# Convolution stem with group norm, forward and gradients: the operand tiles of the input gradient turned by DMA for the weight gradient

## The chip, the cores and the metric

One core of a Trainium2 chip runs the whole program. The metric is the device time of one launch in microseconds (us), for which several runs give a median. A profile shows one execution in detail: TensorE (PE) does the matmuls, with weight loads (PEld) beside them; VectorE (DVE), ScalarE (ACT) and GpSimd (POOL) do the rest; SyncE (SP) does nothing but issue DMA transfers, one after another, and the waits ahead of each. SPq in a profile row is SP's instruction queue; the length of such a row is the time that SP needs to issue the transfer, not the transfer.

## The reference

A strided convolution (31 taps, stride 2, 256 to 256 channels, 2 x 16000 positions), a normalisation over the positions of each channel, GELU, and the gradients of all four inputs:

```python
B, T, D, K = 2, 16000, 256, 31
def _fwd_reference(x, w, gn_gamma, gn_beta):
    s = 2
    L = (T - K) // s + 1
    h = jnp.einsum('blc,cd->bld', x[:, 0:s * L:s, :], w[0])
    for i in range(1, K):
        h = h + jnp.einsum('blc,cd->bld', x[:, i:i + s * L:s, :], w[i])
    mu = jnp.einsum('bld->bd', h)[:, None, :] / L
    var = jnp.einsum('bld->bd', (h - mu) ** 2)[:, None, :] / L
    h = (h - mu) / jnp.sqrt(var + 1e-5)
    h = h * gn_gamma[None, None, :] + gn_beta[None, None, :]
    return _gelu(h)
def reference(x, w, gn_gamma, gn_beta, grad_out):
    _out, _vjp = jax.vjp(_fwd_reference, x, w, gn_gamma, gn_beta)
    return (_out, *_vjp(grad_out))
```

The outputs are out_0 (the activations), out_1 (gradient of x), out_2 (gradient of w), out_3 and out_4 (of gamma and beta).

## The kernel before

All three convolutions (forward, input gradient, weight gradient) are done by a fast algorithm that splits a product of two pairs into three products, A, B_ and C_, of sums or differences of operands, three levels deep. A first-level choice is called a branch (`br`), the second a leaf (`lf`); the third lies inside the matmul groups.

The stages follow one another on TensorE: the forward (L815), the input gradient (L1363), the weight gradient (L1653). GELU and its derivative (`gelu_batch`) of one batch run beside the convolutions of the other.

The input gradient (`input_grad`, L1423) runs over 2 batches, 4 chunks of 512 positions of the folded gradient, 3 branches and 2 halves (`pr`) of a chunk. For a chunk, `e_load` fetches dy and h, `e_comp` makes the gradient rows `EG` out of them, and `e_spread` copies them into `ET` with the margins. `g_sums` builds the operands of a branch on DVE: `first` makes the branch's two rows in `GS`, `second` the leaves A and C_ in `GL` (two buffers, used by turns), `third` and `outer` the third level. Chunks from (0, 3) on take `split` (36 matmuls of 512 columns for each branch and half), the earlier ones `plain` (44).

The weight gradient (`weight_grad`, L1738) goes through nine combinations of branch and leaf (`COMBOS`). Each takes four tiles of x (`x_tile`, 1 MB) and one tile of gradient rows for each batch (`d_tile`, `D2`, with rows as partitions and channels as columns, so the transposed form of what the input gradient uses). These rows are prepared during the input gradient: `dn_turn` (L1311) turns `EG` by two DMA transposes of 512 KB for each chunk and stores the result to `dn_d`; `d2_piece` (L1533) loads pieces of `dn_d` back, forms the first- and second-level differences on DVE (`sub`, L1549) and stores them to `d2_d`, from which `d_tile` loads.

The order of all work is worked out before the launch by `Plan`: every operation is recorded with an engine, an estimated length and what it depends on; two passes give it a due time, to which `self.lead` adds a number for each kind of operation, and a list schedule gives every engine's program order. Each engine, SP too, then executes its list strictly in that order. The estimate for a DMA transpose on SP is in `turn` (L612):

```python
np_ = nbytes / 256
add("SP", 0.15 + 0.00105 * np_, [out], [in_],
    lambda: nc.sync.dma_start_transpose(out=out, in_=in_), dma=np_ * PK[256] / 16e3 * 1.03, ns=PK[256], tp=SH[256], slack=slack)
```

A transpose of 256 KB is issued by `gelu_unit` (two for each unit of batch 0), and one of 32 KB by `dgb_store` for the gradients of gamma and beta. Nearly all DMA transfers go through SP, whether the code says SP or POOL (`load`, L602, sends everything over 4 KB there).

Of the kernel before, what the change touches and what calls it, by code (L numbers as in the profile page):

```python
# [21 lines left out]
ORDER = (B_, A, C_)  # L22
COMBOS = ((A, A), (A, C_), (A, B_), (C_, B_), (B_, B_), (B_, A), (B_, C_), (C_, A), (C_, C_))
# [15 lines left out]
class Plan:  # L39
# [3 lines left out]
    def __init__(self, tc):  # L43
# [11 lines left out]
            "F0 conv_stem_kernel wrapper": 5.6,  # L55
            "F0 f_evac last": -3.2,
            "F0 f_join f_evac": -10.3,
            "F0 f_join split": 14.0,
            "F0 f_mm f_three_ac": -0.4,
            "F0 f_mm f_three_b": 1.0,  # L60
            "F0 f_three_b split": -3.7,
            "F0 keep f_evac": -3.1,
            "F0 keep split": -17.8,
            "F0 load conv_stem_kernel": 58.4,
            "F0 load f_evac": -14.0,
            "F0 load put": 0.6,
            "F0 load x_pre": 3.5,
            "F0 load_gb conv_stem_kernel": -25.1,
            "F0 tt f_sums": -15.0,
            "F0 tt second": 4.0,  # L70
            "F0 tt third": -5.9,
            "F0 turn w2_part": -0.5,
            "F0 turn x_load": -4.6,
            "F0 w_sub w2_part": -5.7,
            "F0 x_pre conv_stem_kernel": 1.3,
            "F0 zero conv_stem_kernel": 0.9,
            "F0 zero f_evac": -7.8,
            "F0 zero w2_part": -33.8,
            "F0 zero x_load": -111.5,
            "F0a f_evac last": -19.8,  # L80
            "F0a f_join f_evac": 0.7,
            "F0a f_join f_first": -11.0,
            "F0a f_join split": 28.3,
            "F0a f_mm f_leaf": -8.4,
            "F0a f_mm f_three_ac": 0.2,
            "F0a f_mm f_three_b": -5.0,
            "F0a f_mm pe_turn": -48.4,
            "F0a f_three_b f_first": -12.7,
            "F0a f_three_b split": -30.8,
            "F0a keep f_first": -31.2,  # L90
            "F0a keep split": -10.0,
            "F0a load load_w": 58.4,
            "F0a load x_load": 82.3,
            "F0a load x_pre": 55.5,
            "F0a put x_first": -19.2,
            "F0a tt f_sums": -12.3,
            "F0a tt second": -19.7,
            "F0a tt third": -13.9,
            "F0a turn x_load": -48.2,
            "F0a w_sub f_first": -12.5,  # L100
            "F0a x_pre conv_stem_kernel": 13.3,
            "F0a zero load_w": 14.3,
            "F1 f_evac last": 4.0,
            "F1 f_join f_evac": 11.4,
            "F1 f_mm f_leaf": 0.7,
            "F1 f_mm f_three_b": 1.8,
            "F1 f_three_b plain": -0.7,
            "F1 f_three_b split": -2.0,
            "F1 gelu_batch conv_stem_kernel": -6.7,
            "F1 gelu_unit gelu_batch": 0.7,  # L110
            "F1 keep f_evac": -0.4,
            "F1 keep plain": -0.3,
            "F1 keep split": -34.2,
            "F1 load f_evac": 0.5,
            "F1 load gelu_unit": 3.0,
            "F1 load out0_store": -3.7,
            "F1 tiny elem_finalize": -260.7,
            "F1 tiny fwd_stats": 2.5,
            "F1 tt f_sums": -15.6,
            "F1 tt second": -1.3,  # L120
            "F1 tt third": 0.6,
            "F1 turn gelu_batch": 0.5,
            "F1 turn gelu_unit": 3.7,
            "F1 turn x_load": 1.8,
            "F1 zero gelu_batch": -52.4,
            "F1z f_evac last": -7.1,
            "F1z f_join f_evac": -5.3,
            "F1z f_join split": -17.5,
            "F1z f_mm f_leaf": -2.5,
            "F1z f_mm f_three_ac": 0.6,  # L130
            "F1z f_mm f_three_b": -0.3,
            "F1z f_three_b split": 2.4,
            "F1z keep f_evac": 7.0,
            "F1z keep split": -160.7,
            "F1z load f_evac": 7.0,
            "F1z tt f_sums": -20.3,
            "F1z tt second": -3.1,
            "F1z tt third": -0.7,
            "F1z turn x_load": 8.8,
            "F1z w_sub f_again": -0.3,  # L140
            "F1z zero f_evac": -10.2,
            "F1z zero x_load": -6.0,
            "G0 e_add e_comp": 3.6,
            "G0 e_comp conv_stem_kernel": -3.2,
# [6 lines left out]
            "G0 g_three_b split": 5.1,  # L151
# [4 lines left out]
            "G0 load e_load": -6.2,  # L156
            "G0 spread e_spread": -288.3,
            "G0 tt first": -2.4,
            "G0 tt outer": 17.1,
            "G0 tt second": -7.8,  # L160
            "G0 tt third": 14.0,
            "G0 turn dn_turn": -10.7,
            "G0 zero e_comp": -37.5,
            "G0 zero e_spread": 69.3,
            "G0a e_add e_comp": -0.5,
            "G0a e_comp conv_stem_kernel": -5.0,
            "G0a e_spread conv_stem_kernel": -1.4,
            "G0a g_join last": -0.9,
            "G0a g_mm g_leaf": 1.6,
            "G0a g_mm g_three_ac": 2.7,  # L170
            "G0a g_mm g_three_b": 2.3,
            "G0a g_three_b plain": 0.6,
            "G0a gelu_batch conv_stem_kernel": -22.1,
            "G0a gelu_unit gelu_batch": 0.3,
            "G0a keep last": 3.8,
            "G0a keep plain": -2.4,
            "G0a load dgb_store": 91.4,
            "G0a load dn_turn": -2.4,
            "G0a load e_load": 11.2,
            "G0a load g_store": 9.1,  # L180
            "G0a load gelu_unit": 4.5,
            "G0a load load_w2": -6.9,
            "G0a spread e_spread": -45.7,
            "G0a tiny elem_finalize": -2.2,
            "G0a tiny fwd_stats": -186.8,
            "G0a tt first": 20.5,
            "G0a tt gelu_unit": -0.6,
            "G0a tt second": -4.2,
            "G0a tt third": 1.7,
            "G0a turn dgb_store": -3.7,  # L190
            "G0a turn gelu_batch": -1.8,
            "G0a w_sub w2_sub": 2.0,
            "G0a zero conv_stem_kernel": -104.8,
            "G0a zero e_spread": -148.7,
            "G0a zero gelu_batch": -5.4,
            "G1 e_add e_comp": -0.5,
            "G1 e_comp conv_stem_kernel": 1.5,
            "G1 e_spread conv_stem_kernel": 0.2,
            "G1 g_join last": 1.0,
            "G1 g_join split": 4.3,  # L200
            "G1 g_mm g_three_ac": -2.1,
            "G1 g_mm g_three_b": -0.3,
            "G1 g_three_b split": -150.3,
            "G1 keep last": -1.0,
            "G1 keep split": 1.0,
            "G1 load d2_piece": 0.8,
            "G1 load dn_turn": -4.2,
            "G1 load e_load": -1.5,
            "G1 spread e_spread": 0.2,
            "G1 sub d2_piece": 0.3,  # L210
            "G1 tt first": 2.1,
            "G1 tt outer": 6.2,
            "G1 tt second": 7.7,
            "G1 tt third": 8.8,
            "G1 turn dn_turn": 0.4,
            "G1 zero e_comp": -0.2,
            "G1 zero e_spread": -0.6,
            "G1z g_join last": -4.0,
            "G1z g_join split": -7.1,
            "G1z g_mm g_three_b": 4.9,  # L220
            "G1z g_three_b split": 5.3,
            "G1z keep split": 7.7,
            "G1z load g_store": 15.8,
            "G1z tt first": -1.8,
            "G1z tt outer": 23.1,
            "G1z tt second": -0.8,
            "G1z tt third": -0.3,
            "W keep w_done": -6.2,
            "W keep weight_grad": -417.1,
            "W leaf_d weight_grad": -3.3,  # L230
            "W load d_tile": 1.3,
            "W load w_done": -3.6,
            "W load w_out": 16.2,
            "W load weight_grad": -11.1,
            "W load x_raw": 16.8,
            "W load x_tile": 6.5,
            "W pair_d weight_grad": 1.6,
            "W pair_x weight_grad": 0.5,
            "W w_add weight_grad": 1.8,
            "W w_add x_tile": -5.4,  # L240
            "W w_mm w_pairs": -3.1,
            "W w_mm w_single": -13.7,
            "W w_pairs weight_grad": -117.4,
            "W w_sum w_done": 3.8,
            "Wa keep w_done": 24.4,
            "Wa keep weight_grad": -116.9,
            "Wa leaf_d weight_grad": -12.3,
            "Wa load d_tile": 22.3,
            "Wa load out0_late": 20.9,
            "Wa load x_raw": 2.8,  # L250
            "Wa pair_d weight_grad": -4.4,
            "Wa pair_x weight_grad": -7.3,
            "Wa turn out0_late": -45.0,
            "Wa w_add weight_grad": 19.2,
            "Wa w_mm w_pairs": -39.5,
            "Wa w_mm w_single": -2.9,
            "Wa w_pairs weight_grad": 10.2,
            "Wa w_sum w_done": 24.8,
# [269 lines left out]
def conv_stem_kernel(  # L528
# [13 lines left out]
    nc = tc.nc  # L542
# [875 lines left out]
    def w2_outer():  # L1418
        for lf in (A, C_):
            for br in ORDER:  # L1420
                w2_sub(MIR[br], MIR[lf])
# [507 lines left out]
```

## Time and profile before

| what | us |
|---|---|
| median of the runs | 1114.31 (1112.18 to 1119.1) |
| profiled execution | 1114.1 |
| its span | 1112.1 |
| PE / DVE / ACT busy | 1082.7 / 993.1 / 609.6 |
| input gradient, first to last matmul begins | 412.2 to 819.1 |
| weight gradient | 819.8 to 1107.7 |

The page's slices of the span (40 of 27.8 us each; a digit is the busy share in tenths):

```profile
PE   5999999999999999999999998999999999999998
...
DVE  6995958789998997999999979979689989999996
...
DMA  9589999976969799889775999999789555796883
```

TensorE is busy nearly everywhere but in the first slice. The chain that ended last is short, since PE rarely waited for anything: its pieces are the last matmuls and the eviction after them.

### The profile page before, as it was taken

The page shows a single profiled execution, that of the slowest core. Times are in us where ns is not written, and L with a number is a line of the kernel's source. Part 1 is how long each engine was busy: PE and PEld are TensorE (multiplying, and loading weights), DVE is VectorE, ACT ScalarE, POOL GpSimd, SP SyncE. Part 2 cuts the span into 40 slices and gives each one's busy share as a digit, 9 for nine tenths or more (in the row PEclk, how much of TensorE's full clock was granted, in tenths as well). Part 3 has the DMA queues.
Part 4 walks back from the last instruction along what each step waited for, and adds up shares of the span by engine and source line. Part 5 has one row for each costly group of instructions (what it writes and reads, how often), then busy time and mean ns, then how long its engine had stood idle before and what let it go on. Part 6 is the DMA issues. An engine that isn't in the chain of part 4 may idle for free. (4 is left out here: it accounts for less than half of the span.)

```text
span 1112.1 us, 19739 instructions
## 1 busy us (share of the span) xinstructions
PE 1082.7 (97%) x8132; PEld 796.3 (72%) x8132; DVE 993.1 (89%) x1026; ACT 609.6 (55%) x854; POOL 11.0 (1%) x27
## 2 busy tenths in 40 slices
PE   5999999999999999999999998999999999999998
PEld 4888889988888984444444443444468888888887
DVE  6995958789998997999999979979689989999996
ACT  2253434588887659797866766665642323322332
POOL 0000000000000000000000000000000000000000
PEclk9999999999999999999999999999999999999999
DMA  9589999976969799889775999999789555796883
GB/s 227 66 220 225 242 272 272 253 151 167 190 202 186 204 334 313 203 254 276 191 245 159 280 330 295 289 301 311 247 277 270 181 194 146 262 333 205 277 255 101
DMA packets 346893, 261.47 MB, mean 235 GB/s; under 512 B 187702, under 2 KB 315572, under 8 KB 340916
## 3 DMA queue, kind: packets, MB, share of 16 engines
q1 hardware_dynamic: 346612, 260.22, 83.8%
q8 instruction: 63, 1.03, 0.4%
q14 instruction: 26, 0.21, 0.1%
q0 software_dynamic: 192, 0.00, 0.0%
HBM read 120.00 MB, written 94.86 MB: 193 GB/s over the span
## 5 line engine op out<-in xcount | busy, mean ns | idle before, releaser
L815 PE MATMUL ps<-arena 128*128 128x256 bf16 (+3 forms) x3668 | 397.7, 272 | 14.6 <-DMA arena<-in_x_dram 6.2
L1363 PE MATMUL ps<-arena 128*128 128x512 bf16 (+1 forms) x1872 | 401.0, 376 | 6.3 <-ACT arena L868 6.1
L815 PEld LDWEIGHTS <-arena 128*128 128x128 bf16 x3668 | 359.9, 99 | 52.2 <-DMA arena<-in_x_dram 6.4
L1363 PEld LDWEIGHTS <-arena 128*128 128x128 bf16 x1872 | 183.2, 98 | 223.8 <-issue 8.9
L868 ACT ACTIVATE arena<-ps 128x1024 bf16<-128x1024 f32 x189 | 191.7, 1022 | 238.8 <-PE ps L1653 123.2
L1653 PE MATMUL ps<-arena 128*128 128x256 bf16 x2592 | 284.2, 273 | 4.3 <-DVE arena L1607 4.3
L1653 PEld LDWEIGHTS <-arena 128*128 128x128 bf16 x2592 | 253.2, 98 | 35.5 <-DVE arena L1607 5.0
L783 DVE TENSOR_TENSOR arena<-arena 128x2064 bf16<-128x2064 bf16 (+7 forms) x132 | 164.7, 1270 | 24.6 <-PE ps L815 19.1
L1607 DVE TENSOR_TENSOR arena<-arena 128x4096 bf16<-128x4096 bf16 (+2 forms) x50 | 107.5, 2178 | 2.7 <-DMA arena<-d2d 2.7
L1167 DVE TENSOR_TENSOR arena<-arena 128x2048 bf16<-128x2048 bf16 (+1 forms) x80 | 95.6, 1198 | 8.9 <-ACT arena L1159 4.6
L1326 DVE TENSOR_TENSOR arena<-arena 128x1032 bf16<-128x1032 bf16 (+7 forms) x111 | 86.4, 803 | 6.7 <-PE ps L1363 5.1
L1390 ACT ACTIVATE ps<-ps 128x512 f32<-128x512 f32 x108 | 63.1, 587 | 34.8 <-PE ps L1363 34.6
L1616 DVE TENSOR_TENSOR arena<-arena 128x4096 bf16<-128x4096 bf16 x32 | 72.6, 2296 | 5.4 <-DMA arena<-in_x_dram 4.0
L1155 ACT ACTIVATE arena<-arena,stats 128x1024 bf16<-128x1024 bf16 (+1 forms) x64 | 75.1, 1209 | 0.8 <-DVE stats L1101 0.8
L1405 DVE TENSOR_TENSOR arena<-arena 128x1024 bf16<-128x1024 bf16 (+1 forms) x70 | 63.3, 919 | 7.1 <-ACT arena L868 7.0
L1549 DVE TENSOR_TENSOR arena<-arena 128x1536 bf16<-128x1536 bf16 (+3 forms) x56 | 61.9, 1128 | 8.0 <-DMA d2d<-arena 5.4
L844 ACT ACTIVATE ps<-ps 128x512 f32<-128x512 f32 x59 | 34.4, 583 | 62.1 <-PE ps L815 62.0
L1725 ACT COPY ps<-ps 128x512 f32<-128x512 f32 x54 | 30.8, 570 | 64.9 <-PE ps L1653 64.9
L1712 DVE TENSOR_TENSOR arena<-arena 128x2048 bf16<-128x2048 bf16 x54 | 64.8, 1232 | 1.1 <-DMA arena<-d2d 1.1
L768 DVE TENSOR_TENSOR arena<-arena 128x2048 bf16<-128x2048 bf16 (+1 forms) x45 | 50.8, 1151 | 16.4 <-DMA arena<-in_w_dram 9.6
L890 ACT ACTIVATE arena<-ps 128x512 bf16<-128x512 f32 (+1 forms) x64 | 36.8, 582 | 37.5 <-PE ps L815 27.7
L1659 DVE TENSOR_TENSOR arena<-arena 128x1024 bf16<-128x1024 bf16 x75 | 49.6, 699 | 6.8 <-ACT arena L868 6.8
(68 smaller groups left out, 464.3 us busy)
## 6 DMA issues: line engine op xcount, KB each, us to landing
arena<-in_x_dram SPq DMA_DIRECT2D x28, 1024.0 KB, 9.5
arena<-d2d SPq DMA_DIRECT2D x16, 1216.0 KB, 8.1
out_dram<-arena SPq DMA_DIRECT2D x35, 512.0 KB, 4.6
d2d<-arena SPq DMA_DIRECT2D x30, 384.0 KB, 6.2
arena<-dnd SPq DMA_DIRECT2D x10, 960.0 KB, 6.4
arena<-vl SPq DMA_DIRECT2D x9, 1024.0 KB, 12.2
arena<-in_x_dram SPq DMA_DIRECT2D x32, 256.0 KB, 4.4
hd<-arena SPq DMA_DIRECT2D x8, 1024.0 KB, 5.6
```

What stands on the lines that cost most here:

```text
L783: lambda: nc.vector.tensor_tensor(out=o, in0=a, in1=b, op=ALU.add))
L815: yield nc.tensor.matmul(ps[:, dh, cs], lhsT=wt, rhs=mv, start=s0, stop=False, skip_group_check=True)
L868: lambda: nc.scalar.activation(out=out, in_=ps, func=ACT.Copy, scale=scale))
L1155: lambda o=o, func=func, i=h[:, dh], sc=sc, bi=bi: SC.activation(out=o, in_=i, func=func, bias=bi, scale=sc))
L1167: add("DVE", dve(8 * wd), [o], [a, b_], lambda: V.tensor_tensor(out=o, in0=a, in1=b_, op=op))
L1326: lambda: nc.vector.tensor_tensor(out=o, in0=a, in1=b, op=ALU.add))
L1363: yield nc.tensor.matmul(ps[:, e, 0:wide], lhsT=lt, rhs=mv, start=s0, stop=False, skip_group_check=True)
L1405: add("DVE", dve(o.free_size(), rate), [o], [a, b], lambda: nc.vector.tensor_tensor(out=o, in0=a, in1=b, op=op))
L1607: add("DVE", dve(o.free_size()), outs, ins, lambda: nc.vector.tensor_tensor(out=o, in0=a, in1=b, op=op), kind=kind + " weight_grad")
L1616: add("DVE", dve(4096), [o], [a, b], lambda: nc.vector.tensor_tensor(out=o, in0=a, in1=b, op=ALU.add))
L1653: yield nc.tensor.matmul(ps[:, s, c0:c1], lhsT=lt, rhs=mv, start=s0, stop=False, skip_group_check=True)
L1712: add("DVE", dve(2048), [d4], [d], lambda: nc.vector.tensor_tensor(out=d4, in0=fan(d[:, o0:o0 + 3 * s + 1:s, :], 1, (o1 - o0) * D), in1=fa ...
```

## The change

The gradient rows of the weight gradient are no longer made from a transposed copy of `EG`. Instead each operand tile that `g_sums` has made for the input gradient (the leaf tiles `pl` of a branch: rows of `ET` or `GS`, and both leaves of `GL`) is turned by DMA as it stands and stored straight to `d2_d`. Sums stand there where differences stood, so the x operands become differences (`w_diff`), and some sums of the results in `w_done` change sign. `dn_turn`, `d2_piece`, `dn_d` and their buffers go; the branches of the input gradient run in the order B_, C_, A (`GORD`). Two x tiles change places, so that the tiles of a pair lie side by side, and the leads are set anew, nearly all of them (two lines stand for the table below).

```diff
-            "G0 keep split": -156.4,
...
-            "G0 load dn_turn": 15.0,
...
+            "G0 keep split": -122.1,
...
+            "G0 load d2_turn": 0.4,
...
-    def dn_turn(b, c, o):
-        for dh in range(2):
-            turn(o.rearrange("p r a d -> p (r a) d")[:, :, dh * P:(dh + 1) * P],
-                 EG[:, dh].rearrange("p e k f -> p (e k f)"), 524288)
-        r0 = (192 if b else 0) + 2048 * c + 15
-        for a in range(2):
-            load(dn_d[b][r0 + 1024 * a:r0 + 1024 * a + 1024, :].rearrange("(p r) d -> p r d", r=8), o[:, :, a, :], 524288, 512, "POOL")
+    d2c = [0]
+    DT = [sb(GREG + 12800 + 2048 * i, 2, 2, D) for i in range(4)]
+
+    def d2_row(b, i, r, ap):
+        v = d2_d[b][i][:]
+        return bass.AP(tensor=v.tensor, offset=v.offset + r * D, ap=ap)
+
+    def d2_turn(b, c, br, lf, v):
+        t = DT[d2c[0] % len(DT)]
+        d2c[0] += 1
+        i = 3 * MIR[br] + MIR[lf]
+        for j in range(2):
+            for dh in range(2):
+                turn(t[:, :, j, dh * P:(dh + 1) * P], v[:, dh, j, 1:257], 65536)
+        r = 512 * c + (50 if b else 2)
+        if (b, c) == (1, 3):
+            for f, n in ((0, P), (1, 105)):
+                load(d2_row(b, i, r + 256 * f, [[2 * D, n], [1, 2 * D]]), t[0:n, f].rearrange("p j d -> p (j d)"), n * 1024, 1024, "POOL")
+        else:
+            load(d2_row(b, i, r, [[2 * D, P], [256 * D, 2], [1, 2 * D]]), t.rearrange("p f j d -> p f (j d)"), 262144, 1024, "POOL")
...
                     for pr in range(2):
                         (split if (b, c) in GV else plain)(b, c, pr, br, P * pr, sums)
+                        if pr == 0:
+                            for lf in ORDER:
+                                d2_turn(b, c, br, lf, sums[6][lf])
...
-            w_add(t, t, XT_[j])
+            w_diff(t, XT_[j], t)
...
-    XT_ = [sb(o, 8, 512) for o in (24576, 32768, 40960, 49152)]
+    XT_ = [sb(o, 8, 512) for o in (24576, 40960, 32768, 49152)]
...
-            for z in ((dn_d[0][8207:8207 + 128, :], zt2[:, 0:256]), (dn_d[1][0:128, :], zt2[:, 0:256]),
-                      (dn_d[1][128:207, :], zt2[0:79, 0:256]), (dn_d[0][0:15, :], zt2[0:15, 0:256])):
-                load(z[0], z[1], 65536, 512, "POOL", slack=300.0)
+            for i in range(9):
+                for b_, r, n in ((0, 0, 2), (0, 2050, 1), (1, 0, 50)):
+                    load(d2_row(b_, i, r, [[D, n], [1, D]]), zt2[0:n, 0:256], 512 * n, 512, "POOL", slack=300.0)
...
-            dn_turn(*nxt, DNO)
...
-        if (b, c, br, pr) in D2AT:
-            plan.hold = plan.npe
-            for pc in D2AT[b, c, br, pr]:
-                d2_piece(0, pc)
```

SP's order before, where the last chunk's h and dy (`hd_3`, `dyd_3`) are loaded during the input gradient of batch 1; `dnd` is `dn_d`, `d2d` is `d2_d`:

```order
L610 DMA dnd_81<-arena 1024x1x256 x2
L610 DMA d2d_86<-arena 128x2x768
L610 DMA arena<-dnd_80 128x2816
L610 DMA d2d_86<-arena 128x2x768
L610 DMA out_dram<-arena 512x1x512
L610 DMA arena<-hd_3_67 128x4096
L610 DMA arena<-dyd_3_75 128x4096
L610 DMA d2d_86<-arena 128x2x768
```

And SP's order now at the same loads:

```order
L621 DMA d2d_7_100<-arena 128x2x512
L626 DMA_TRANSPOSE arena<-arena 128x2x128 x8
L621 DMA out_dram<-arena 512x1x512
L621 DMA arena<-hd_3_67 128x4096
L626 DMA_TRANSPOSE arena<-arena 128x2x128 x4
L621 DMA d2d_8_101<-arena 128x2x512
L621 DMA d2d_6_99<-arena 128x2x512
L626 DMA_TRANSPOSE arena<-arena 128x2x128 x4
L621 DMA arena<-dyd_3_75 128x4096
```

The loads now have eight small turns ahead of them and eight more between them. The second place is the end of the input gradient on SP, where the first gradient tiles of the weight gradient (128x4864) and its x tiles (128x8x512) are loaded. Before:

```order
L610 DMA arena<-d2d_86 128x4864
L610 DMA d2d_87<-arena 128x2x512 x2
L610 DMA out_dram<-arena 512x1x512
L610 DMA arena<-in_x_dram 128x8x512
L610 DMA arena<-d2d_87 128x4864
L610 DMA arena<-in_x_dram 128x8x512
```

Now:

```order
L626 DMA_TRANSPOSE arena<-arena 128x2x128 x2
L621 DMA arena<-in_x_dram 128x8x512
L621 DMA d2d_0_93<-arena 105x512
L626 DMA_TRANSPOSE arena<-arena 128x2x128 x6
L621 DMA out_dram<-arena 512x1x512
L621 DMA d2d_8_101<-arena 128x512
L621 DMA d2d_8_101<-arena 105x512
L621 DMA d2d_6_99<-arena 128x512
L621 DMA d2d_6_99<-arena 105x512
L621 DMA arena<-d2d_0_93 128x4864
L621 DMA out_dram<-arena 512x1x512
L621 DMA arena<-in_x_dram 128x8x512 x2
```

The second gradient tile and the last x tiles of the first combination stand behind the last of the 288 turns and their stores. PE's list has the same 8132 matmuls in both, and DVE's loses the 56 differences of `d2_piece` and nothing else.

More of the change, by code (lines that the diff above doesn't have):

```diff
@@ L67, in __init__ @@
[L67 to L79, printed above, removed]
@@ L183, in __init__ @@
[L183 to L195, printed above, removed]
@@ L214, in __init__ @@
[L214 to L219, printed above, removed]
+            "G1 keep split": 0.7,
+            "G1 load d2_turn": -0.9,
+            "G1 load e_load": -16.8,
+            "G1 load g_store": -6.7,
+            "G1 spread e_spread": -7.1,
+            "G1 tt first": -12.3,
+            "G1 tt outer": -7.3,
+            "G1 tt second": 6.3,
```

452 lines of the change are left out of this document (222 added, 230 removed).

## The prediction

> **What bounds the kernel now.** I read the page's first part, then the table of stretches (forward; input gradient 412 to 820; weight gradient to 1108), then the wait list, and last the sync queue's own rows.
>
> ```profile
> PE 1082.7 (97%) x8132; PEld 796.3 (72%) x8132; DVE 993.1 (89%) x1026; ACT 609.6 (55%) x854; POOL 11.0 (1%) x27
> ...
> 0.00:28.00 28.00, 15.39 (x106) 11.39 (x106) 17.25 (x24) 5.90 (x7) 1.76 (x9) 1.00 1.02 225
> 28.00:412.00 384.00, 382.01 (x3564) 348.41 (x3562) 332.27 (x358) 226.28 (x367) 5.33 (x9) 1.00 0.88 213
> 412.00:820.00 408.00, 401.37 (x1878) 183.53 (x1876) 367.37 (x437) 291.77 (x373) 3.39 (x8) 1.00 0.89 266
> 820.00:1108.00 288.00, 283.96 (x2592) 252.93 (x2590) 274.94 (x209) 85.62 (x108) 0.53 (x1) 1.00 0.71 224
> ...
> PE ps L1363 <- ACT arena L868: 6.1, 4, 3.8
> ```
>
> Columns of a stretch: its bounds, its length, then busy time of PE, weight load, DVE, ACT and POOL, the granted clock (1.00 throughout) and the DMA share. TensorE is busy 1082.7 of 1112.1 us. The change issues the same 8132 multiplications, so at most 29.4 us can be won: 12.6 before 28 us, 2.0 in the forward, 6.6 in the input gradient, 4.0 in the weight gradient, and 4 after 1108, where the outputs drain. The input gradient, where the change sits, has 6.6 us to give. Any large effect must therefore be a loss: something that is hidden beside those 408 us and grows longer than they are.
>
> **What the change takes away.** The differences of `d2_piece` leave VectorE:
>
> ```profile
> L1549 DVE TENSOR_TENSOR arena<-arena 128x1536 bf16<-128x1536 bf16 (+3 forms) x56 | 61.9, 1128 | 8.0 <-DMA d2d<-arena 5.4
> ...
> 629.00:676.00 47.00, 46.06 (x215) 20.90 (x214) 39.91 (x46) 29.14 (x42) 0.00 (x0) 1.00 0.99 285
> 676.00:724.00 48.00, 44.15 (x206) 19.95 (x205) 42.75 (x56) 33.50 (x48) 0.00 (x0) 1.00 0.97 305
> 724.00:772.00 48.00, 46.92 (x220) 21.36 (x219) 41.70 (x43) 29.92 (x41) 1.18 (x3) 1.00 0.95 302
> ```
>
> 56 instructions, 61.9 us. They lie beside matmuls, so what they are worth is the PE idle time in the three stretches where they crowd: 0.9 + 3.9 + 1.1 = 5.9 us, of which I count all as gained if nothing else binds. The bytes fall too: before, by the sizes in the code, 8.4 MB are turned and as many stored to `dn_d`, 12.7 MB read back and 19.9 MB stored to `d2_d` (49.4 MB); now 18.9 MB are turned and 18.7 MB stored (37.6 MB). So I cost the DMA engines, at a share of 0.89 in this stretch, at nothing. The 27 zero stores instead of four go early, 18 of them from POOL (11.0 us busy in the whole run) and nine from SP: nothing. Sums that became differences keep shape and count: nothing. The new places of the x tiles leave the number of instructions as it was: nothing.
>
> **What the change puts in.** 72 operand tiles (8 chunks, 3 branches, 3 leaves) are turned by four DMA transposes of 64 KB each: 288 turns, where `dn_turn` had 16 of 512 KB. All stand on SP, which issues one DMA after another in a fixed order, with the loads of the next chunk, the stores of out_1 and the first loads of the weight gradient between them. So the price of one issue counts, and the rows are:
>
> ```profile
> L615 SPq DMA_TRANSPOSE arena<-arena x16: 1182/2536/5120, 411.4 to 740.8; - x16
> ...
> L615 SPq DMA_TRANSPOSE arena<-in_grad_out_dram x16: 1507/2882/6254, 206.6 to 562.1; - x16
> ...
> 274.54 1.26 SPq L615 DMA_TRANSPOSE arena<-arena  x1
> ...
> 453.63 1.79 SPq L615 DMA_TRANSPOSE arena<-arena  x1
> ...
> 740.38 0.39 SPq L610 DMA_DIRECT2D d2d<-arena  x1
> 740.82 1.18 SPq L615 DMA_TRANSPOSE arena<-arena  x1
> ```
>
> The turn at 274.54 is one of 256 KB (`gelu_unit`), that at 453.63 one of 512 KB (`dn_turn`), that at 740.82 the 32 KB of `dgb_store`, which is also the 1182 ns minimum. From 256 KB to 32 KB the price falls only from 1.26 to 1.18: it is nearly all fixed. A 64 KB turn lies between these two sizes, so I take 1.19 us, and 0.05 of gap to the next issue (740.38 + 0.39 to 740.82). The other end of the range is the straight line through 512 KB (1.79) and 256 KB (1.26): 0.53 per 256 KB, hence 0.86 at 64 KB; the 32 KB row speaks against it, and it is the only small one. Above, 1.26. The planner's own formula in `turn` counts 0.42 us for such a turn; no row supports it, and the order was laid out with it.
>
> The rest of what SP issues in the stretch:
>
> ```profile
> L610 SPq DMA_DIRECT2D d2d<-arena x70: 359/466/2355, 612.7 to 797.2; - x70
> L610 SPq DMA_DIRECT2D out_dram<-arena x31: 534/563/1743, 446.0 to 818.7; - x31
> ...
> L610 SPq DMA_DIRECT2D arena<-hd x13: 325/587/1241, 432.6 to 686.1; - x13
> L610 SPq DMA_DIRECT2D yd<-arena x8: 397/402/1076, 434.9 to 572.2; - x8
> L610 SPq DMA_DIRECT2D dyd<-arena x8: 519/572/1390, 441.4 to 581.0; - x8
> L610 SPq DMA_DIRECT2D arena<-dyd x7: 418/864/1594, 420.6 to 688.2; - x7
> L610 SPq DMA_DIRECT2D arena<-in_x_dram x7: 599/695/3382, 719.1 to 812.5; - x7
> L610 SPq DMA_DIRECT2D arena<-vl x3: 540/713/4633, 421.2 to 429.5; - x3
> ```
>
> From the first leaf turn to the load of the second `D2` tile of the weight gradient, the new order has 449 issues: 288 turns; 81 stores to `d2_d` (x 0.47 = 38); 28 of out_1 (x 0.56 = 16); 13 loads of h, 6 of dy, 8 stores of y, 8 of dy, 3 of w2, 3 of x, one store of h and one load of `d2_d` (together 26 at the medians); 8 turns of grad_out (x 2.9 = 23); the one of `dgb_store` (1). With 0.05 of gap for each plain DMA (8) that is 112 us at these medians and 83 at the minima of the same rows (0.36 for a `d2_d` store, 1.5 for a grad_out turn, and so on); SP's rows are longer than their minima where the queue is full, and I take the middle, 98. The turns: 288 x 1.24 = 357. Sum 455 us. The multiplications that it runs beside last 408.
>
> **On the path.** The first leaf is ready about when the input gradient begins, 412, and SP comes to the last load at 412 + 455 = 867. Behind that load stand:
>
> ```profile
> arena<-in_x_dram SPq DMA_DIRECT2D x28, 1024.0 KB, 9.5
> ...
> L1607 DVE TENSOR_TENSOR arena<-arena 128x4096 bf16<-128x4096 bf16 x22 | 50.4, 2296 | 0.0
> ...
> L1607 DVE TENSOR_TENSOR arena<-arena 128x2048 bf16<-128x2048 bf16 x10 | 12.0, 1228 | 0.0
> ...
> 819.81 12.39 PE L1653 MATMUL ps<-arena 128*128 128x256 bf16 x112 [0.30 <-DVE arena L1607]
> ```
>
> the last x tile (9.5 us to landing), its sum (2.3) and the pairs (1.2): 13 us. So the first matmul of the weight gradient comes at 880 instead of 819.8: 60 us later. The profiled execution took 1114.1 us (span 1112.1), the median of the runs shown is 1114.31, so no correction: 1114 + 60 = 1174. The 5.9 us that VectorE could give are lost in that.
>
> How the lateness spreads before that: the turns read `GL`, `ET` and `GS`, so the sum that refills a `GL` buffer two branches later (`second`, on DVE) now waits for SP's turns, and behind it in DVE's queue stand the joins that free PSUM, for which PE waits. In the first three chunks SP has also the GELU of batch 1 to serve, and a split chunk needs 36 x 1.24 + 9 x 0.52 + 4 x 0.61 + 2 x 0.6 = 53 us of SP beside its 216 matmuls, some 47 us of PE (215 in the 47 us from 629 to 676 above). PE's idle time should thus appear all along the stretch, not only at its end.
>
> The skill's rule that bears on this is in the Trainium skill, "DMA: Bandwidth & Descriptors", section "Rules for kernel authors": many small transfers should be joined, since under 64 KB one pays mostly overhead. The rows above agree for the issue of a turn (1.18 us at 32 KB, 1.26 at 256 KB).
>
> **Rivals.**
> *A small turn is cheap (R1).* If the line of 0.86 us holds, SP needs 288 x 0.91 + 98 = 360 us, comes to the last load at 772 and the x tile's sum is there at 785, before 819.8. All is hidden; the gain is at most the 5.9 us, the loss a few us where the fixed order makes SP late in the crowded first chunks: 1108 to 1122, say 1112. For it: the 512 KB and 256 KB rows. Against it: the 32 KB row, and that it leaves SP 88% full. It decides below 288 x (T + 0.05) = 820 - 13 - 412 - 98 = 297, that is T = 0.98 us.
> The Trainium skill, "Advanced Engine Details and Errata", section "X-Bar Transpose (TRN2)", says that transposing DMAs are as fast as regular ones. By that a turn would issue like a plain store, and R1 would hold; in the rows here a plain store of 128 KB or more issues in 0.36 to 0.47 us and no turn in less than 1.18, so the issue, at least, does not follow it.
> *VectorE's relief wins (R2).* With T below 0.98 and the 61.9 us gone, PE loses its 6.6 us of idle time in the stretch and, with new leads, part of the 4.0 in the weight gradient: 1114 - 10 = 1104. It would need more than that, 11 us, to be faster by over 1%. For it: DVE is 90% busy (367 of 408). Against it: PE waited only 6.1 us for evictions there.
> *The turns block one another (R3).* Turns of 512 KB in this stretch took 2.5 us in the median where a free queue takes 1.79. If a 64 KB turn shares 0.1 of that and the other issues cost their medians, SP needs 288 x 1.34 + 112 = 498, the weight gradient begins at 923 and the time is 1217. For it: the DMA share of 0.89. Against it: an SP that is itself the bound leaves the DMA engines emptier, and fewer bytes move.
>
> **How the numbers follow.** Forecast (SP's issue of 288 turns longer than the stretch, 1125 to 1200): 0.66. R3: 0.07. R1: 0.20. R2: 0.07. The time is 1174. With the other issues at both their ends and T from 0.98 to 1.26 the forecast alone spans about 1114 to 1208; the range must reach R1 to leave out no more than 2 in 10: 1106 to 1208. Since the cases lie on both sides, the forecast's own range is 1130 to 1208. A measurement of this kernel can tell about 1% from no change: faster by more than that 0.05 (most of R2), within it 0.23 (R1, the rest of R2, the low end of the forecast), slower 0.72 (the forecast and R3).
>
> **What would show it.** Right: the rows of the 64 KB turns on SP at 1.15 to 1.25 us each and SP's issues following one another without a gap from 420 on; DVE's sums of `g_sums` waiting for DMA transposes; PE idle by 40 us or more between the first and last matmul of the input gradient, and a gap ahead of the weight gradient's first matmul that ends with an x or d load. Wrong: turns of 0.5 to 0.9 us, an SP that waits for VectorE (then it is ahead), the weight gradient beginning near 815 to 820 (R1), or PE's share at 98% (R2). A gap elsewhere, in the forward or within the weight gradient, would say that the new leads did it and not the turns.

## The result and the profile after

The changed kernel takes 1267.9 us (median of four runs, 1264.63 to 1268.21) against 1113.24 for the kernel before on the same chip: a ratio of 1.137, 95% interval 1.133 to 1.142. The prediction said 1174, with a range up to 1208: the direction held, the size did not.

First, parts one and two of the page of the changed kernel: busy times, the row of the granted clock in 40 slices, and the DMA share in the same slices.

```profile
PE 1112.0 (88%) x8094; PEld 803.1 (63%) x8132; DVE 941.4 (74%) x970; ACT 610.6 (48%) x854; POOL 20.0 (2%) x45
...
PEclk9999999999999897879988988879789999999999
DMA  9689999879979756686694745565558765579775
```

TensorE was 97% busy and is now 88%. The clock, full everywhere before, dips between slices 14 and 30, and the DMA engines are emptier there. The table of stretches shows that all of it lies in the input gradient. Columns: bounds, length, busy time of PE, weight load, DVE, ACT, POOL, granted clock, DMA share, GB/s.

```profile
28.00:412.00 384.00, 382.93 (x3563) 348.60 (x3565) 334.42 (x361) 226.06 (x367) 14.93 (x28) 1.00 0.89 214
412.00:960.00 548.00, 415.72 (x1758) 183.12 (x1792) 303.79 (x369) 284.06 (x363) 2.75 (x7) 0.88 0.63 167
960.00:1262.00 302.00, 299.00 (x2663) 260.09 (x2663) 285.60 (x218) 95.18 (x120) 0.53 (x1) 1.00 0.72 230
```

The forward and the weight gradient run as before. From the first matmul of the input gradient to the first of the weight gradient it took 408 us (412.2 to 819.8) and now takes 565 (410.4 to 975.4; the table cuts it at 412 and 960). In it PE, DVE, ACT and the DMA engines are all less busy per microsecond. Only the sync queue isn't. These are the rows of its instructions in the changed kernel from 409 to 957 us: number, then shortest, median and longest issue in ns.

```profile
L626 SPq DMA_TRANSPOSE arena<-arena x289: 1167/1244/2797, 409.8 to 950.2; - x145
L626 SPq DMA_TRANSPOSE arena<-in_grad_out_dram x8: 1692/3734/11703, 429.5 to 653.6; - x8
...
L621 SPq DMA_DIRECT2D d2d<-arena x81: 328/584/2312, 428.3 to 954.3; - x81
L621 SPq DMA_DIRECT2D out_dram<-arena x28: 547/572/1021, 471.8 to 951.5; - x28
L621 SPq DMA_DIRECT2D arena<-hd x13: 519/587/921, 426.4 to 826.4; - x13
```

Added up over all rows from 409.8 to the load of the second `D2` tile at 956.4, they stand beside the terms of the forecast like this (us):

```
                                    forecast   measured
288 leaf turns, dgb_store's turn        344      379.6   (mean 1.313)
8 turns of grad_out                      18       35.5   (mean 4.43)
153 plain transfers                      71       92.8
gaps and semaphores                      22       39.2
SP, first leaf turn to last load        455      547
```

How SP spends its time shows in a piece of its timeline in the changed kernel (start, length, instruction, number of them):

```profile
547.61 0.53 SPq L621 DMA_DIRECT2D dyd<-arena  x1
548.20 5.01 SPq L626 DMA_TRANSPOSE arena<-arena  x3
553.25 0.59 SPq L621 DMA_DIRECT2D d2d<-arena  x1
554.27 0.59 SPq L621 DMA_DIRECT2D arena<-hd  x1
554.91 4.40 SPq L626 DMA_TRANSPOSE arena<-in_grad_out_dram  x1
559.36 1.24 SPq L626 DMA_TRANSPOSE arena<-arena  x1
...
956.37 0.33 SPq L621 DMA_DIRECT2D arena<-d2d  x1
```

One issue follows the other; from 420 to 940 the rows fill 92 to 97% of each 20 us, but for those that begin at 500 (75%), 680 (83%) and 900 (86%). A load that stands in this list comes when its turn comes. Where that hurts is in the wait list of the changed kernel for 412 to 960 us (who waits, for whom: us in total, times, longest):

```profile
PEld L1387 <- issue: 178.1, 176, 16.5
PE ps L1387 <- ACT arena L879: 84.7, 12, 16.2
DVE arena L1429 <- ACT arena L879: 67.1, 29, 16.4
ACT arena L1166 <- DMA arena<-hd: 57.6, 6, 20.1
...
ACT arena L879 <- DMA out_dram<-arena: 52.4, 7, 17.6
...
DVE arena L1274 <- DMA arena<-dyd: 28.7, 4, 12.2
```

ScalarE's evictions (L879) wait for stores of out_1 that free their buffers, its GELU (L1166) for loads of h, VectorE (L1274) for loads of dy: all of these are ordinary transfers that stand behind turns in SP's list. TensorE then waits for the evictions. Against this, the rows of the input gradient's matmuls on the two pages, the changed kernel first, then the kernel before:

```profile
L1387 PE MATMUL ps<-arena 128*128 128x512 bf16 (+1 forms) x1834 | 432.7, 397 | 132.4 <-ACT arena L879 84.7
```

```profile
L1363 PE MATMUL ps<-arena 128*128 128x512 bf16 (+1 forms) x1872 | 401.0, 376 | 6.3 <-ACT arena L868 6.1
```

Idle time ahead of them grew from 6.3 to 132.4 us (+126), and their busy time by 31.7 at the lower clock, though 38 records are missing. Together that is 158, about the 155.6 by which the first matmul of the weight gradient moved (819.8 to 975.4). So about four fifths of the loss is waiting, and a fifth is matmuls that run at a lower clock while there is waiting.

### The profile page after: what moved, and what is told of

Read it like the earlier page. It is cut to its first block, busy times and chain, and to the rows that moved or that the text cites. A ratio compares the mean times of both kernels' runs of the same rounds, so it can differ in the third digit from the quotient of the medians.

```text
span 1266.4 us, 19974 instructions
## 1 busy us (share of the span) xinstructions
PE 1112.0 (88%) x8094; PEld 803.1 (63%) x8132; DVE 941.4 (74%) x970; ACT 610.6 (48%) x854; POOL 20.0 (2%) x45
## 5 line engine op out<-in xcount | busy, mean ns | idle before, releaser
L1387 PE MATMUL ps<-arena 128*128 128x512 bf16 (+1 forms) x1834 | 432.7, 397 | 132.4 <-ACT arena L879 84.7
L879 ACT ACTIVATE arena<-ps 128x1024 bf16<-128x1024 f32 x189 | 191.5, 1022 | 316.3 <-PE ps L1631 115.0
L794 DVE TENSOR_TENSOR arena<-arena 128x2080 bf16<-128x2080 bf16 (+7 forms) x132 | 163.8, 1267 | 37.9 <-PE ps L826 19.2
L1178 DVE TENSOR_TENSOR arena<-arena 128x2048 bf16<-128x2048 bf16 (+1 forms) x80 | 95.6, 1196 | 30.5 <-ACT arena L1172 20.3
L1585 DVE TENSOR_TENSOR arena<-arena 128x4096 bf16<-128x4096 bf16 (+2 forms) x50 | 107.3, 2166 | 0.2
L1166 ACT ACTIVATE arena<-arena,stats 128x1024 bf16<-128x1024 bf16 (+1 forms) x64 | 75.2, 1210 | 63.0 <-DMA arena<-hd 57.6
L1694 DVE TENSOR_TENSOR arena<-arena 128x2048 bf16<-128x2048 bf16 x54 | 64.1, 1217 | 0.3 <-PE ps L1387 0.2
L928 DVE TENSOR_TENSOR arena<-arena 128x1024 bf16<-128x1024 bf16 (+3 forms) x52 | 43.6, 841 | 8.4 <-ACT arena L901 5.1
L1168 DVE SCALAR_TENSOR_TENSOR arena<-arena 128x2048 bf16<-128x2048 bf16 (+1 forms) x16 | 35.8, 2239 | 14.8 <-ACT arena L1166 14.8
```

What stands on the lines that cost most here:

```text
L794: lambda: nc.vector.tensor_tensor(out=o, in0=a, in1=b, op=ALU.add))
L879: lambda: nc.scalar.activation(out=out, in_=ps, func=ACT.Copy, scale=scale))
L1166: lambda o=o, func=func, i=h[:, dh], sc=sc, bi=bi: SC.activation(out=o, in_=i, func=func, bias=bi, scale=sc))
L1178: add("DVE", dve(8 * wd), [o], [a, b_], lambda: V.tensor_tensor(out=o, in0=a, in1=b_, op=op))
L1387: yield nc.tensor.matmul(ps[:, e, 0:wide], lhsT=lt, rhs=mv, start=s0, stop=False, skip_group_check=True)
L1585: add("DVE", dve(o.free_size()), outs, ins, lambda: nc.vector.tensor_tensor(out=o, in0=a, in1=b, op=op), kind=kind + " weight_grad")
```

## The experiments

The theory after the result: SP's issue price of a turn hardly depends on its size, SP is the bound of the stretch, and the time follows the number of issues. Rivals: the turned bytes; the new order, laid out with a wrong price; the other parts of the change. In the runs named half, no and three quarters, all other instructions stand in the places of the changed kernel; what isn't turned there, and in `half_cols`, is stored as zeros, so their out_2 is not the whole result and only their time counts. Each ratio is to the kernel before as it ran beside that run (medians of 1111.5 to 1116.6 us). "Start" below is the first matmul of the weight gradient in the run's profile.

```
run              turns in the stretch        start   median us  ratio to before, 95%
no_turns         0                           809.9   1100.7     0.988 [0.985, 0.991]
half_turns       144 of 64 KB                826.5   1118.2     1.003 [1.001, 1.006]
three_quarters   216 of 64 KB                891.3   1182.2     1.063 [1.060, 1.065]
after            288 of 64 KB                975.4   1267.9     1.137 [1.133, 1.142]
half_cols        288 of 32 KB                971.1   1264.5     1.135 [1.130, 1.139]
true_price       288 of 64 KB, new order     975.1   1289.5     1.157 [1.149, 1.165]
stores_pool      288 of 64 KB                953.7   1250.0     1.121 [1.117, 1.124]
one_turn         72 of 256 KB                834.0   1127.3     1.011 [1.009, 1.014]
before           16 of 512 KB                819.8   1113.2     1
before_split8    128 of 64 KB                913.0   1207.4     1.083 [1.080, 1.086]
before_split16   256 of 32 KB                1073.6  1366.4     1.225 [1.222, 1.228]
```

**Half the columns, and half the turns.** `half_cols` keeps 288 turns and halves their bytes; `half_turns` keeps their size and halves their number.

```diff
-                turn(t[:, :, j, dh * P:(dh + 1) * P], v[:, dh, j, 1:257], 65536)
+                half_turn(t[:, 0:1, j, dh * P:(dh + 1) * P], v[:, dh, j, 1:129], t[:, :, j, dh * P:(dh + 1) * P], v[:, dh, j, 1:257])
...
```

```diff
-                turn(t[:, :, j, dh * P:(dh + 1) * P], v[:, dh, j, 1:257], 65536)
+                half_turn(dh == 0, t[:, :, j, dh * P:(dh + 1) * P], v[:, dh, j, 1:257], t[:, :, j, dh * P:(dh + 1) * P], v[:, dh, j, 1:257])
...
```

`half_turn` issues the turn (in the second diff only where its first argument is true) and gives the planner the old operands, length and bytes, so that the order stays.

> The changed kernel with its 288 turns, each over 128 of its 256 columns (32 KB instead of 64 KB; the other half of each tile stays zero in the stores), in the same order on every engine. If a turn costs SP a fixed time for its issue: the turns' rows stay at 1.18 to 1.25 us, SP needs nearly as long as now (547 us from the first turn to the load ahead of the weight gradient), total 1230 to 1268. If the turned bytes are the cost (crossbar or DMA engines): half of 377 us of turns goes, the stretch is hidden again, total 1115 to 1150. If the order with its waits is the cost: 1255 to 1275.

> The changed kernel with only the 144 turns of the first channel half (64 KB each; the other half of each tile stays zero in the stores), in the same order on every engine otherwise. The bytes turned are those of the kernel with half columns. If the issue count is the cost: SP needs 547 - 144 x 1.37 = 350 us, less than the 408 us of matmuls, total 1105 to 1135, with 64 KB turns still at 1.2 to 1.3 us each. If bytes are the cost: the same time as the kernel with half columns. If the order is the cost: above 1200.

Rows of the turns, `half_cols` first, then `half_turns`:

```profile
L1331 SPq DMA_TRANSPOSE arena<-arena x288: 1093/1231/2893, 409.6 to 945.8; - x144
```

```profile
L1331 SPq DMA_TRANSPOSE arena<-arena x144: 1167/1243/2583, 409.3 to 792.8; - x144
```

The median issue of 32 KB is 1.231 us, that of 64 KB 1.243: the bytes don't matter. With half the bytes in as many turns the time is 3 us of the loss of 155 lower, which lies within the intervals; half the turns saved nearly all of it. The bytes fall as a cause, the count stands.

**No turns.** The condition `dh == 0` above becomes `False`; the stores of the rows stay.

> The changed kernel without its 288 turns (the stores write zeros), all else in the same order. Tells what the other parts of the change are worth: stores to d2_d, leads, branch order, the differences that leave VectorE. If the turns are the whole loss: 1098 to 1115, TensorE's idle time in the input gradient at or under the 6.6 us of before, and its granted clock back at 1.0. If leads or stores carry a part of the loss, what stands above 1115 is theirs.

1100.7 us: everything else that the change does (VectorE freed of the differences, no reading back, none of the 16 old turns, new leads) is worth about 13 us. The turns cost 167 and are the whole loss.

**The right price in the planner.** One line, and the order of everything is laid out anew with it:

```diff
-        add("SP", 0.15 + 0.00105 * np_, [out], [in_],
+        add("SP", max(1.37, 0.15 + 0.00105 * np_), [out], [in_],
```

> The changed kernel, its order laid out anew with a turn counted at no less than 1.37 us on SP instead of 0.42 (same leads, same work, complete). If SP's need is the cost: 449 issues still take 520 to 550 us, total 1235 to 1270. If the order laid out with too low a price is the cost: most of the loss goes, total under 1180.

The start comes at 975.1, as with the wrong price, though the last matmuls of the input gradient are done at 947.6. The rows of PE there:

```profile
975.06 1.04 PE L1631 MATMUL ps<-arena 128*128 128x256 bf16 x4 [27.48 <-DVE arena L1585]
992.38 7.82 PE L1631 MATMUL ps<-arena 128*128 128x256 bf16 x56 [16.29 <-DMA arena<-d2d]
```

PE waits 27.5 us for an x sum (L1585): SP issues an x load at 963.5, right ahead of the last leaf turn at 964.1. So the queue is no shorter in this order, and part of the waiting stands in another place. Most of the 22 us that the run is slower than the changed kernel is the next wait, 16.3 us for a `D2` load. The leads are those set with the wrong price; leads set anew with the right one were not tried.

**Stores from another queue.** The 81 stores to `d2_d` leave SP for GpSimd (their calls pass "GP" in place of "POOL"):

```diff
-        if nbytes > 4096:
+        if nbytes > 4096 and eng != "GP":
             eng = "SP"
+        eng = eng.replace("GP", "POOL")
...
```

> The changed kernel with the 81 stores of turned rows to d2_d issued by GpSimd instead of SP; all 288 turns stay, the order is laid out anew. Theory (the stretch lasts as long as SP needs): SP loses 81 x (0.625 + 0.05) = 55 us of its 547, the weight gradient begins near 920 instead of 975, and the time is 1213 (1195 to 1235). Rival (SP is busy only because it waits in line for the DMA engines): the same bytes through another queue change nothing, 1255 to 1285. Rival (the stretch is bound by the chain turn, store, load of a leaf): the same, or longer, since GpSimd issues more slowly.

Relief of SP helps, but by 18 us, a third of what was expected. The wait list of this run from 412 to 960 us:

```profile
POOL d2d L622 <- DMA arena<-arena: 453.9, 61, 27.6
PEld L1388 <- issue: 152.0, 168, 10.8
PE ps L1388 <- ACT arena L880: 51.1, 9, 10.5
```

GpSimd does nothing but wait for turns, so no room there was missing; but the turns themselves grew (mean 1.361, +14 us over 288) and SP now waits 15 us on semaphores, 12 more than in the changed kernel. From the first turn to the load of the second `D2` tile SP still took 522 us against 547. The size expected was wrong because a saved store is partly paid back by longer turns and by waits for what is to be turned.

**The kernel before, with its turns split.** No part of the change is in these two; each 512 KB turn of `dn_turn` goes out in 16 pieces, one behind the other (the diff), or in 8 (`16 // 8` and `range(8)`). The planner still sees one turn, so the order stays.

```diff
+    def split_turn(out, in_):
+        def go():
+            n = 16 // 16
+            for i in range(16):
+                yield nc.sync.dma_start_transpose(out=out[:, n * i:n * i + n], in_=in_[:, 128 * n * i:128 * n * i + 128 * n])
...
-            turn(o.rearrange("p r a d -> p (r a) d")[:, :, dh * P:(dh + 1) * P],
-                 EG[:, dh].rearrange("p e k f -> p (e k f)"), 524288)
+            split_turn(o.rearrange("p r a d -> p (r a) d")[:, :, dh * P:(dh + 1) * P],
+                       EG[:, dh].rearrange("p e k f -> p (e k f)"))
```

> The kernel before, with each of the 16 turns of 512 KB in dn_turn issued as 16 turns of 32 KB: 256 turns, the same bytes, the same order, nothing else of the change. Theory (a nearly fixed issue price of 1.3 us on SP): 256 x 1.35 = 346 us in place of 42, so SP needs 209 + 11 + 304 = 525 us beside the 408 of the input gradient: the weight gradient begins 90 to 125 us later, 1205 to 1240. Rival (the price goes by bytes): 1114 to 1120. Rival (the loss needs the new leaves, their waits or the new order): 1114 to 1125.

> The kernel before, with each of the 16 turns of 512 KB in dn_turn issued as 8 turns of 64 KB: 128 turns, the same bytes and order. Theory: 128 x 1.35 = 173 us in place of 42, so SP needs 209 + 11 + 131 = 351 of 408 us: nearly hidden, 1114 to 1130; far below half of the loss of 256 turns, since only what exceeds the stretch counts. Rival (each turn costs its issue time wherever it stands): half the loss of 256 turns, 1160 to 1175.

The same bytes in more turns cost 93 and 252 us: more issues make a loss by themselves, without leaves, without new leads. But both are worse than the theory said, and the expectation that 128 turns are nearly hidden fell outright. SP was not full there: with 8 pieces its rows fill 77% of 412 to 820 us, and still the start moves by 93. The timeline of SP in `before_split8` shows how the turns stand there:

```profile
575.60 0.59 SPq L610 DMA_DIRECT2D arena<-hd  x1
578.30 21.68 SPq L1315 DMA_TRANSPOSE arena<-arena  x16
600.08 0.53 SPq L610 DMA_DIRECT2D yd<-arena  x1
600.71 0.58 SPq L610 DMA_DIRECT2D out_dram<-arena  x1
```

And two of its waits, 412 to 1060 us:

```profile
PE ps L1370 <- ACT arena L868: 63.7, 13, 11.4
ACT arena L868 <- DMA out_dram<-arena: 45.2, 7, 14.8
```

The two turns of a chunk, 5.0 us of SP before (at 545.83), are now a block of 21.7 us, and the out_1 stores behind it come late; ScalarE waits for buffers (45.2 us; 8.4 in the kernel before, 412 to 820), then TensorE for ScalarE (63.7; 6.1 before). So a block can delay what stands behind it even if the queue has time left over the whole stretch. In `half_turns`, 144 turns that are spread over the queue cost 17 us against none; the 128 turns of this kernel were not run spread out, so that the blocks do it is argued from these waits. Between 8 and 16 pieces, 128 more turns cost 159 us, 1.24 each and so their issue time, though SP's rows fill only 76% of 412 to 1060 us there.

**One turn for each leaf.** The leaves are copied into contiguous tiles and turned by one instruction of 256 KB. Four runs differ in who copies and in the order.

```diff
+    CT = [[sb(o + 2048 * i, 2, 2, 2, P) for i in range(3)] for o in (148416, GREG)]
...
-        for j in range(2):
-            for dh in range(2):
-                turn(t[:, :, j, dh * P:(dh + 1) * P], v[:, dh, j, 1:257], 65536)
+        ct = CT[int((b, c) in GV)][d2c[0] % 3]
+        add("DVE", dve(1024, 4), [ct], [v], lambda: nc.vector.tensor_copy(out=ct, in_=v[:, :, :, 1:257].rearrange("p e j (f c) -> p f j e c", f=2)), kind="turn d2_turn")
+        turn(t.rearrange("p f j (e c) -> p (f j e) c", e=2), ct.rearrange("p f j e c -> p (f j e c)"), 262144)
```

> The whole computation, with 72 turns of 256 KB in place of 288 of 64 KB; VectorE first copies each leaf into a contiguous tile (72 copies of 128 x 1024), and the order is laid out anew. Theory (SP's issue of the turns is the whole loss): SP saves 216 issues of 1.3 us with their gaps, some 290 us of the 547 it needed, so it is hidden again; the turns now cost what they cost without any issue time, and the time is that of the run without turns, 1101, plus what the copies cost VectorE: 1100 to 1112, below the kernel before (1114). Rival (the bytes or the later stores bind): the same 18.9 MB are turned and stored, so the time stays near 1268. Rival (VectorE becomes the bound through the copies, some 40 us beside 408): 1120 to 1140.

This takes 141 us of the loss back: 1127.3. Its turns in the profile from the first on:

```profile
L626 SPq DMA_TRANSPOSE arena<-arena x73: 1232/1286/4367, 418.8 to 801.2; - x73
```

A turn of 256 KB issues in 1.286 us in the median, one of 64 KB in 1.244. Four times the data cost 0.04 us of SP in the median (in the mean 1.610 against 1.313). The run does not reach the 1101 to 1112 expected, and three more runs asked why.

> The whole computation; one 256 KB turn for each leaf as in the run one_turn, with the 72 copies on ScalarE instead of VectorE (about 1.0 us each by the 128 x 1024 copies in the profile, 72 us), the order laid out anew. Theory (the 12 us that one_turn lost to the kernel before are VectorE's crowding: a wait of 9.4 us of TensorE for g_sums and the slower clock behind it): 1101 to 1113, at or below the kernel before. Rival (DMA traffic early in the stretch, a share of 1.05 to 1.12 from 420 to 460, cost it): as one_turn, 1122 to 1132. Rival (ScalarE, 295 us busy in 408 without the copies, becomes the next bound): 1125 to 1150.

> The whole computation; as one_turn, with the 72 copies on GpSimd, which has 11 us of work in the kernel before. Theory (VectorE's crowding): 1101 to 1112. Rival (a copy on GpSimd takes several us, or slows VectorE beside it): turns come late behind the copies, 1125 to 1200.

With the copies on ScalarE 1159.2 us (1.038 [1.035, 1.041]), on GpSimd 1150.4 (1.030 [1.027, 1.033]): both worse, and the gain that the theory of a crowded VectorE promised did not come. They don't rule it out, since a copy takes 1.04 us on ScalarE and 1.69 on GpSimd against 0.42 on VectorE. Both runs also lose time where nothing was changed: PE is busy 374.48 and 371.94 of the 384 us of the forward, where the changed kernel has 382.93. Each has a new order; whether it is the order that costs the forward some 10 us is not shown.

> The whole computation; as one_turn (72 copies on VectorE, 72 turns of 256 KB), but in the order of the changed kernel: the work of every engine stands as there, each copy where the first of the leaf's four turns stood and the turn where the fourth stood. Theory (a new layout of the order cost one_turn its 26 us over the run without turns, since moving the copies off VectorE made it worse, not better): 1100.7 of the run without turns, plus 30 us of copies on a VectorE that is about 80% busy, of which a fifth to a third can reach TensorE: 1101 to 1112, below the kernel before. Rival (the 72 turns themselves or the copies cost it, in any order): 1120 to 1135.

1127.9 us (1.012 [1.010, 1.014]). In this order the copies' tiles lie in memory that other work still uses, so the run computes something else, and its copies wait 15.7 us, nearly all for DMA transfers; the outcome is as the rival said, but it doesn't settle it. What the 27 us between `no_turns` and `one_turn` are stays open: the copies, the turns of the first chunks beside the GELU of batch 1, or the order. No version run here beats the kernel before with the whole computation.

**Three quarters of the turns.** This puts SP's need where the forecast had it.

> The changed kernel with 216 of the 288 turns (of each leaf's four, the one for the second halves of rows and channels is left out; its part of the stored rows is zeros), every instruction else in its place. Theory (time follows SP's total need in the stretch, as the prediction's sum had it): SP needs 547 - 72 x (1.314 + 0.045) = 449 us, about the 455 that the prediction took; the last load goes out at 410 + 449 = 859, the weight gradient begins 19 us later at 878, and 292 us after that the end: 1171 (1155 to 1185). Rival (each added turn costs the same, a line from 144 turns, 1118, to 288, 1268): 1193 (1187 to 1200). Rival (the loss comes only with the last turns, when some buffer runs out): below 1140.

SP needed 460 us here, from 409 to the load at 868.5, and the weight gradient began at 891.3: 1182.2 us. The forecast took 455 us of SP and said 1174.

## Why the prediction was right or wrong

- **SP's queue as the bound, with a nearly fixed price of a turn: right.** Shown by `half_cols` (bytes halved, same time), `half_turns`, `no_turns` and the split turns of the kernel before. The rule of the Trainium skill, "DMA: Bandwidth & Descriptors", "Rules for kernel authors", that small transfers should be joined, agrees: 72 turns in place of 288 took 1268 to 1127.
- **The ledger "Sum 455 us": the step that failed.** Measured 547; the mechanism was right and the terms were too small. The turn was put at 1.19 us, between the best cases of two sizes; the rows have 1.167 as their minimum, 1.244 as their median and 1.313 as their mean (+36). The turns of grad_out and the plain transfers were put at the middle of median and minimum and came out above the medians (+18 and +22). Gaps and semaphores were more (+17). A sum needs means. Those of the trace before would have served for two of the terms: there a turn of grad_out takes 3.96 us in the mean and a store to `d2_d` 0.606 (median 0.466), which makes 32 and, over all plain transfers, 104 us, where 35.5 and 92.8 were measured. That SP was half idle in that trace (its rows fill 51% of 412 to 820) was thus not the fault. For the turn of 64 KB that trace had no row. That `three_quarters`, whose SP really needed 460, took 1182 shows that the way from SP's need to the time was sound, and the need was too small.
- **Why the mean of a turn lies above its median** is only in part shown. A fuller queue does not make it larger: in `half_turns`, where the rows fill 81% of the time from 409 to 815 us, the mean is 1.373. The long turns mostly stand behind plain transfers: in the changed kernel a turn right behind one takes 1.455 us in the mean (63 of them), one right behind another turn 1.274 (222); in `half_turns` it is 1.463 and 1.307. What a plain transfer does to the turn behind it stays open.
- **"13 us" behind the last load: 19 measured** (956.4 to 975.4; in `three_quarters` 22.8). A small part of the miss.
- **How the lateness spreads: half right.** PE idles all along the stretch, as said. But the sums of `g_sums` hardly wait for turns; the rows of who waited for L626 in the changed kernel:

```profile
  DVE arena L1350: 3.1, 2
  DVE arena L1178: 1.2, 1
```

It went through the loads of h and dy and the stores of out_1 behind the turns instead.
- **The clock: not foreseen.** It was taken as full; with idle gaps it was 0.88 in the mean, and the matmuls took 397 ns instead of 376.
- **Gains taken as lost: right.** They exist (13 us in `no_turns`; the prediction had 5.9 plus whatever the leads give) but don't show beside the queue.
- **R1 (a small turn is cheap) is out**: no turn of 64 KB took less than 1.167 us. With it falls, for the issue, the rule that transposing DMAs are as fast as regular ones (the Trainium skill, "Advanced Engine Details and Errata", "X-Bar Transpose (TRN2)"): in the changed kernel a turn of 64 KB holds SP for 1.244 us in the median, a `d2_d` store of mostly 256 KB for 0.584.
- **R2 (VectorE's relief wins) is out**, since PE's idle time grew. **R3 (turns block one another)** had 1.34 us with gap and the others at medians; the measured 1.36 with gap is close to it, but even its 1217 was too low, because the other transfers cost more than their medians and SP had more gaps and waits. The reason given for it, a DMA share of 0.89, does not fit: in the changed kernel it was 0.63 in the stretch.
- **Break-even at T = 0.98 us: not tested as a price**, but the count that just hides lies near 144 turns: from 0 to 144 a turn costs 0.12 us (17.5 in all), from 144 to 216 0.89, from 216 to 288 1.19, near the median issue time of 1.244.

## What to carry to other kernels

Add up the issue time of the one queue that carries everything, in the stretch where it must be done, with mean durations and not with minima or medians, since a few long issues add to the sum and don't show in a median. Count DMA transposes by number and not by bytes, and join them. A queue with time to spare over a stage can still delay it, as the split turns did, where blocks of issues stood in front of stores that free buffers.

## What was unexpected of the hardware

- The issue of a DMA transpose between buffers on the chip is nearly flat in size up to 256 KB: medians of 1.231 us at 32 KB, 1.244 at 64 KB, 1.286 at 256 KB (means 1.301, 1.313, 1.610). At 512 KB it isn't: the median of the 16 rows of the kernel before, nearly all of that size, is 2.536.
- The granted clock falls where TensorE has gaps, and matmuls take longer then (397 against 376 ns): it is 0.88 in the stretch of the changed kernel, 0.93 in `three_quarters`, 0.99 in `half_turns`, 1.00 in `no_turns`, each for 412 to 820 us:

```profile
412.00:820.00 408.00, 309.78 (x1316) 136.75 (x1341) 247.83 (x304) 222.09 (x279) 1.53 (x4) 0.88 0.66 173
```

```profile
412.00:820.00 408.00, 353.44 (x1570) 157.68 (x1569) 278.60 (x343) 254.88 (x325) 2.74 (x7) 0.93 0.73 192
```

Behind the mean stand two values. Cut where the clock changes, rows of the changed kernel show half and full clock:

```profile
433.10:443.10 10.00, 3.35 (x8) 1.13 (x8) 7.06 (x10) 4.42 (x5) 0.00 (x0) 0.50 1.05 334
443.30:484.10 40.80, 37.12 (x173) 17.13 (x175) 30.16 (x35) 27.04 (x31) 0.00 (x0) 1.00 0.56 153
```

Half clock holds for 95.6 of the 408 us from 412 to 820, which makes the mean of 0.88. The Trainium skill, "TensorE: Matmul & The Clock Gate", "Part 1: The HAM clock gate (the "warmup" mystery)", lists two states, half after at least one idle window of some 3.4 us and full after a busy one. The trace agrees with the two values, 0.50 and 1.00; how long a window is was not measured here.
